# When the second layer's weight sums are made, and where its first outputs are copied, in an attention and two-MLP kernel

## The chip, the cores and the metric

The kernel runs on 1 core of one Trainium2 chip. The metric is the device time of one execution in microseconds (us). Engines are named as in the profile: PE (TensorE), DVE (VectorE), ACT (ScalarE), POOL (GpSimd) and SP (SyncE, which here only issues DMAs). Every engine and every DMA queue takes its instructions in the order in which they were laid down.

## The reference

Attention with a forget gate gives 2304 tokens of 512 values. Two MLPs follow, each with a hidden width of 2048:

```
x = attention(q, k, v, s)                          # 4 x 576 tokens, 8 heads of 64
h = x @ w_in1;  g = s1 * relu(h)**2 + b1;  x2 = g @ w_out1
h = x2 @ w_in2; g = relu(h) + alpha * min(h, 0);   out = g @ w_out2
```

## The kernel before

**Numbers.** All matrices are float32 in value. Each operand is split into a high and a low part (`split`: ACT copies the value into a rounded type, the high part; another engine, mostly DVE, subtracts to get the low part), and a product is three matmuls: high by high, high by low, low by high.

**Blocks.** Tokens go through a layer in blocks of 256. `SIZES` joins some: layer 0 (the first MLP) has seven single blocks and a wide one of 512 tokens (its matmuls write `hp` at L771 and `acc` at L882); layer 1 (the second MLP) has one single block, t=0, and then four wide ones, t=1 to 4. Every block has 16 steps f, one for each 128 hidden units: `up(f)` multiplies into PSUM, ACT and DVE apply the non-linear function and split the result into `gh` and `gl` (tiles `ring`), and `down(f)`, which is laid down two steps later in layer 0 and three in layer 1 (`LAG`), accumulates into the banks `acc`. `finish` copies the banks out.

**Packets.** The weights of layer 1 are loaded, converted (L140 on ACT, L141 and L142 on DVE) and split (L130 on ACT, L131 on DVE) in 16 packets while the wide block of layer 0 runs.

**Strassen.** The wide blocks of layer 1 save one product of eight: for two neighbouring steps, f and f+1 (one **pair**; there are 8), `up_first` makes three products in the PSUM banks a, b, c and `up_second` four more. Four of the seven left operands are sums of quarters of the weights. These sums don't depend on the tokens. `make_sums(pair)` makes them once: POOL adds ten times (L727; tiles `sum0` to `sum3`), then each of the four sums is split (ACT copy L130, DVE subtraction L131) into one of two halves of a small room, `rests` (in the rows the tiles `w1_0_0` with `w1_0_1`, and `w1_0_2` with `w1_0_3`), and written to DRAM (`sums_d`, two DMAs of 128 KB for each sum). Sums 0 and 2 share the first half and sums 1 and 3 the second, so each waits for the DMAs of the one ahead of it. `load_sums` brings a pair back into the tiles `sums` (L745, 256 KB for each sum) in every wide block, when `up_first` and `up_second` of the pair ahead have read the old ones.

**The order of the work.** The code is written in a program order, and a scheduler that works with modelled times lays the instructions down on each engine: an instruction may move ahead of others where the model has its operands ready and its engine free. `tc.issue_after(ins)` pins what is made inside it behind `ins` on that instruction's own engine. In program order, before, `make_sums` is called in block t=0 of layer 1 at f = 0, 3, 6, 9, 12, 15 and in block t=1 at f = 0 and 2; no pin holds its splits.

**The non-linear function of layer 1.** ACT makes the positive part `r` and the negative part `u` (tiles with the tags `ph` and `pl`, two buffers each), DVE merges them (`scalar_tensor_tensor`, L795 in block t=0 and L820 in the wide blocks), and `split` follows.

Of the kernel before, what the change touches and what calls it, by code (L numbers as in the profile page):

```python
# [12 lines left out]
AF = mybir.ActivationFunctionType  # L13
ALU = mybir.AluOpType
# [5 lines left out]
def tile_forget_attention__then__two_mlps(  # L20
# [20 lines left out]
    nc = tc.nc  # L41
# [6 lines left out]
    NF = DFF // P  # L48
# [13 lines left out]
    REBASE, W_SCALE = 2.0**-111, 2.0**8  # L62
# [22 lines left out]
    gate_s, gate_b, bsum, nalpha = misc[:, 0:1], misc[:, 1:2], misc[:, 4 : 4 + NCC], misc[:, 8 : 8 + NF]  # L85
# [43 lines left out]
    def split(hi, lo, src, lo_eng=nc.vector):  # L129
        nc.scalar.copy(hi, src)  # L130
        lo_eng.tensor_tensor(out=lo, in0=src, in1=hi.bitcast(F32), op=ALU.subtract)  # L131
# [14 lines left out]
    def slot(n, dtype, name):  # L146
        return wp.tile([P, 512], dtype, tag=f"w{n}", name=name)
# [560 lines left out]
        return {n: [x.rearrange("p (c n) -> p c n", c=2) for x in pair] for n, pair in parts.items()}, None  # L708

    ring, relus = [], []  # L710
    wide_ring, sums, sums_at = [], [], list(range(NF // 2))

    def halves(f):
        return [x.rearrange("p (k n) -> p k n", k=2) for x in (y.rearrange("p c n -> p (c n)") for y in packet(1, f)[:2])]
# [3 lines left out]
    def make_sums(pair):  # L718

        (h1, l1), (h2, l2) = halves(2 * pair), halves(2 * pair + 1)  # L720
        f32 = lambda x: x.bitcast(F32)
        add, sub = ALU.add, ALU.subtract

        def chain(n, first, *rest):
            out = one.tile([P, 2 * P], F32, tag=("ql00", "ql10", "ql11", "ql11")[n], name=f"sum{n}_{pair}")
            for m, (op, x) in enumerate(rest):
                nc.gpsimd.tensor_tensor(out=out, in0=out if m else f32(first), in1=f32(x), op=op)  # L727
            return out

        s1 = chain(0, h2[:, 0], (add, h2[:, 1]), (add, l2[:, 0]), (add, l2[:, 1]))  # L730
        s2 = chain(1, s1, (sub, h1[:, 0]), (sub, l1[:, 0]))
        s3 = chain(2, h1[:, 0], (sub, h2[:, 0]), (add, l1[:, 0]), (sub, l2[:, 0]))
        for n in range(4):
            s = chain(3, h1[:, 1], (sub, s2), (add, l1[:, 1])) if n == 3 else (s1, s2, s3)[n]
            hi, lo = rests[2 * (n % 2) : 2 * (n % 2) + 2]
            split(hi, lo, s)
            for z, part in enumerate((hi, lo)):
                nc.sync.dma_start(out=sums_d[pair, n, :, z * 2 * P : (z + 1) * 2 * P], in_=part.bitcast(F32))

# [8 lines left out]
    def mlp_block(layer, t, x):  # L748
# [5 lines left out]
        first, count = SIZES[layer][t]  # L754
# [5 lines left out]
        def up(f):  # L760
            w = packet(layer, f)
            if layer == 0 and count == 1:
                hp = ps_h.tile([P, 512], F32, tag="hp", name=f"hp{layer}_{t}_{f}")
            else:
                hp = ps.tile([P, 512], F32, tag="b", name=f"hp{layer}_{t}_{f}", bufs=4)
            hs = hp[:, :TB]
            terms = ((w[0], xh), (w[0], xl), (w[1], xh))
            n = 0
            for c in range(NCC):
                for a, b in terms:  # L770
                    nc.tensor.matmul(hs, a[:, c], b[c], start=(n == 0), stop=(n == len(terms) * NCC - 1))  # L771
                    n += 1
            if layer == 0 and count == 2:
                if not wide_ring:
                    tiles = [xfp.tile([P, 4, T], F32R, tag="xf", name=f"ring{n}") for n in range(3)]
                    for z in range(2):
                        wide_ring.append([x[:, 2 * z : 2 * z + 2].rearrange("p z n -> p (z n)") for x in tiles])
                gh, gl = (x[f % 3] for x in wide_ring)
                r = two.tile([P, TB], F32, tag="ph", name=f"r{t}_{f}")
            elif layer == 0:  # L780
                gh = two.tile([P, T], F32R, tag="gh", name=f"gh{layer}_{t}_{f}", bufs=3)
                gl = two.tile([P, T], F32R, tag="gl", name=f"gl{layer}_{t}_{f}", bufs=3)
                r = two.tile([P, T], F32, tag="r", name=f"r{t}_{f}")
            else:
                if not ring:
                    ring.extend([slot(n, F32R, f"ring{n}") for n in SPLIT[m]] for m in free[:2])
                gh, gl = (x[f % 4][:, :TB] for x in ring)
                r = two.tile([P, 512], F32, tag="ph", name=f"r1_{t}_{f}")[:, :TB]
                u = two.tile([P, 512], F32, tag="pl", name=f"u1_{t}_{f}")[:, :TB]
            relus.append(nc.scalar.activation(r, hs, AF.Relu, scale=1.0 / W_SCALE).ins)  # L790
            if layer == 0:
                nc.scalar.square(r, r)
            else:
                nc.scalar.activation(u, hs, AF.Relu, scale=-1.0 / W_SCALE)
                nc.vector.scalar_tensor_tensor(  # L795
                    out=r, in0=u, scalar=nalpha[:, f : f + 1], in1=r, op0=ALU.mult, op1=ALU.add
                )
            split(gh, gl, r, nc.gpsimd if layer == 0 and count == 1 else nc.vector)
            return gh, gl

# [11 lines left out]
        def next_sums(f, which):  # L812
            if f // 2 + 1 < NF // 2 or t + 1 < len(SIZES[1]):
                load_sums((f // 2 + 1) % (NF // 2), which)

        def temp(tag, name, bufs):
            return two.tile([P, T], F32, tag=tag, name=name, bufs=bufs)

        def prelu(r, u, f):
            nc.vector.scalar_tensor_tensor(  # L820
                out=r, in0=u, scalar=nalpha[:, f : f + 1], in1=r, op0=ALU.mult, op1=ALU.add
            )
            gh, gl = (y[f % 4][:, :TB] for y in ring)
            split(gh, gl, r)
            return gh, gl

        def relu_pair(r, u, src):
            nc.scalar.activation(r, src, AF.Relu, scale=1.0 / W_SCALE)
            nc.scalar.activation(u, src, AF.Relu, scale=-1.0 / W_SCALE)  # L829

        def up_first(f):
# [64 lines left out]

        def finish():
            for m, bank in enumerate(banks):
                if layer == 1 and count == 2:
                    res = two.tile([P, 512], F32, tag=("ph", "pl")[m % 2], name=f"res1_{t}_{m}")  # L900
                else:
                    if m % 2 == 0:
                        pool = xfp if m else one
                        both = pool.tile([P, 1024], F32, tag="xf" if m else "res", name=f"res{layer}_{t}_{m}")
                    res = both[:, m % 2 * 512 : (m % 2 + 1) * 512]
                if layer == 0:
                    for z in range(1 if count == 2 else 2):
                        d = m if count == 2 else 2 * m + z
                        dst, src = (res, bank) if count == 2 else (x[:, z * T : (z + 1) * T] for x in (res, bank))
# [4 lines left out]
                        else:  # L914
                            nc.vector.tensor_scalar(
                                out=dst, in0=src, scalar1=gate_s[:, 0:1], scalar2=bsum[:, d : d + 1],
                                op0=ALU.mult, op1=ALU.add,
# [5 lines left out]
                if layer == 0 and count == 2:  # L923
                    nc.sync.dma_start(
                        out=x2_d[first : first + 2, :, m * T : (m + 1) * T].rearrange("z p n -> p z n"),
# [46 lines left out]
    for n in range(len(BLOCKS) * NF):  # L972
# [18 lines left out]
            if n - NF * (len(SIZES[0]) - 1) == at:  # L991
                packet(1, j)
        if layer == 1:
            if sums_at and f % (2 if t else 3) == 0:
                make_sums(sums_at.pop(0))
        while done < len(units) and done < pace((n + 1) / NF):
            next(side, None)
# [39 lines left out]
```

## Time and profile before

| what | value |
|---|---|
| median of 3 runs | 1058.45 us (1057.36 to 1058.65) |
| the profiled execution | 1059.27 us, span 1057.5 us, mean granted clock 0.991 |
| PE busy | 1025.1 us, 97% of the span |
| DVE, ACT, POOL busy | 694.2, 673.9, 480.6 us |

The span runs from the first to the last instruction. Block t=0 of layer 1 begins on PE at 655.4 us of the span, block t=1 at 712.5 us, and its other three wide blocks follow. "idle" is the time for which an engine had nothing running ahead of an instruction, and "<-" names what ended it.

### The profile page before, as it was taken

How to read it: one execution, taken by the hardware profiler on the slowest of the kernel's cores; microseconds unless marked ns; L12 is line 12 of the kernel's file. 1: busy time of each engine (PE TensorE's matmuls, PEld its weight loads, DVE VectorE, ACT ScalarE, POOL GpSimd, SP SyncE). 2: the span in 40 equal slices, each digit the busy share in tenths (PEclk: the TensorE clock that was granted, in tenths of full speed). 3: DMA queues.
4: the chain of work that ended last, by engine and by line, in shares of the span. 5: the costliest groups of instructions: out<-in, count | busy, mean ns of one | idle time of the engine just before them, and what ended most of it. 6: DMA issues, size and time to landing. Idle time of an engine off the chain costs nothing.

```text
span 1057.5 us, 20662 instructions
## 1 busy us (share of the span) xinstructions
PE 1025.1 (97%) x6952; PEld 927.7 (88%) x6952; DVE 694.2 (66%) x1605; ACT 673.9 (64%) x1669; POOL 480.6 (45%) x892
## 2 busy tenths in 40 slices
PE   9899999999999999999999889799999999999997
PEld 4578899999999999999998667699999999999996
DVE  6888864786677766777557997945455446446443
ACT  5877866777778877877766665744454455445443
POOL 6556775666677666776644676512011002000000
PEclk9899999999999999999999999899999999999999
DMA  7998432342234332343126776514334335334331
GB/s 156 246 250 223 118 72 60 82 95 65 50 79 86 92 67 46 78 91 83 46 80 213 234 204 204 169 34 158 101 123 156 101 100 179 101 100 130 110 103 56
DMA packets 197930, 125.45 MB, mean 119 GB/s; under 512 B 138496, under 2 KB 167936, under 8 KB 197824
## 3 DMA queue, kind: packets, MB, share of 16 engines
q1 hardware_dynamic: 193744, 123.56, 42.5%
q8 instruction: 55, 0.90, 0.4%
q10 hardware_dynamic: 4080, 0.57, 0.3%
q14 instruction: 51, 0.42, 0.1%
HBM read 106.19 MB, written 17.90 MB: 117 GB/s over the span
## 4 chain that ended last, share of the span: by engine, by line
PE 76%; DVE 7%; DMA 7%; ACT 4%; issue 3%; POOL 2%; SPq 1%; ACTq 0%; DVEq 0%; POOLq 0%
PE acc L892 19%; PE p L807 15%; PE hp L771 15%; PE acc L882 13%; PE av L531 4%; PE pt L515 4%; PE sc L460 2%; DMA sums_d<-w 1%; DVE w L131 1%; PE sc L459 1%; DVE wt L142 1%; DMA wi<-in_moe_w_in_dram 1%; PE sc L457 1%; DMA wo<-in_moe_w_out_dram 1%; DVE wt L141 1%
## 5 line engine op out<-in xcount | busy, mean ns | idle before, releaser
L771 PE MATMUL hp<-xh,w 128*128 128x256 f32 (+1 forms) x1024 | 229.2, 301 | 0.6 <-ACT r L790 0.6
L892 PE MATMUL acc<-w,ring 128*128 128x512 f32 x864 | 215.6, 394 | 5.8 <-ACT res L911 5.8
L892 PEld LDWEIGHTS acc<-w,ring 128*128 128x128 f32 x864 | 157.6, 190 | 34.8 <-ACT res L911 6.0
L771 PEld LDWEIGHTS hp<-xh,w 128*128 128x128 f32 x1024 | 171.6, 190 | 6.6 <-ACT r L790 1.0
L882 PE MATMUL acc<-gh,w 128*128 128x256 f32 x896 | 172.3, 286 | 0.6 <-ACT res L911 0.5
L771 PE MATMUL hp<-xl,w 128*128 128x256 f32 (+1 forms) x512 | 152.6, 298 | 0.0
L868 POOL TENSOR_TENSOR cc<-u,t 128x256 f32<-128x256 f32 x32 | 25.7, 802 | 277.9 <-DVE u L859 241.6
L882 PEld LDWEIGHTS acc<-gh,w 128*128 128x128 f32 x896 | 136.0, 189 | 3.3 <-issue 1.3
L882 PE MATMUL acc<-gl,w 128*128 128x256 f32 x448 | 118.7, 288 | 1.4 <-POOL gl L131 1.4
L484 POOL TENSOR_SCALAR probs<-probs,sm 64x64 f32<-64x64 f32 (+4 forms) x160 | 91.3, 584 | 61.0 <-DVE sm L481 50.6
L473 ACT ACTIVATE probs<-probs,nm 64x64 f32<-64x64 f32 (+4 forms) x160 | 90.0, 563 | 37.8 <-DVE nm L461 26.1
L131 POOL TENSOR_TENSOR gl<-r,gh 128x256 fp32r<-128x256 f32 x112 | 89.5, 799 | 50.8 <-ACT gh L130 44.0
L807 PE MATMUL p<-xs,sums 128*128 128x256 f32 x768 | 103.9, 282 | 0.0
L771 PEld LDWEIGHTS hp<-xl,w 128*128 128x128 f32 x512 | 97.3, 190 | 3.4 <-issue 0.4
L807 PEld LDWEIGHTS p<-xs,sums 128*128 128x128 f32 x768 | 97.6, 189 | 1.0
L461 DVE CUSTOM_DVE_ANT_0 probs<-sc,probs 128x320 f32<-128x320 f32 (+3 forms) x160 | 68.2, 427 | 42.3 <-PE sc L460 27.7
L790 ACT ACTIVATE r<-hp 128x256 f32<-128x256 f32 (+1 forms) x144 | 58.0, 403 | 41.9 <-PE hp L771 31.3
L882 PEld LDWEIGHTS acc<-gl,w 128*128 128x128 f32 x448 | 80.1, 188 | 4.1 <-issue 2.0
L807 PEld LDWEIGHTS p<-xs,w 128*128 128x128 f32 x576 | 78.7, 189 | 5.4
L807 PE MATMUL p<-xs,w 128*128 128x256 f32 x576 | 81.3, 282 | 0.0
L515 PE MATMUL pt<-ident,probs 128*128 128x128 f32 x480 | 75.1, 277 | 4.2 <-POOL probs L484 2.4
L820 DVE SCALAR_TENSOR_TENSOR ph<-pl,misc,ph 128x512 f32<-128x512 f32 x64 | 48.6, 759 | 38.3 <-ACT pl L829 38.3
(149 smaller groups left out, 2160.7 us busy)
## 6 DMA issues: line engine op xcount, KB each, us to landing
sums<-sums_d SPq DMA_DIRECT2D x128, 256.0 KB, 2.7
wi<-in_moe_w_in_dram SPq DMA_DIRECT2D x32, 512.0 KB, 5.2
wo<-in_moe_w_out_dram SPq DMA_DIRECT2D x32, 512.0 KB, 5.3
cum<-cum_d SPq DMA_DIRECT2D x32, 288.0 KB, 3.7
sums_d<-w SPq DMA_DIRECT2D x64, 128.0 KB, 3.2
cum<-cum_d SPq DMA_DIRECT2D x30, 160.0 KB, 3.1
nat<-in_k_dram SPq DMA_DIRECT2D x64, 72.0 KB, 2.5
x_d<-res SPq DMA_DIRECT2D x18, 256.0 KB, 2.2
```

What stands on the lines that cost most here:

```text
L131: lo_eng.tensor_tensor(out=lo, in0=src, in1=hi.bitcast(F32), op=ALU.subtract)
L461: nc.vector.tensor_tensor_reduce(out=pt[:rows, j0:j1], in0=scr, in1=pt[:rows, j0:j1], scale=SCALE if flip else -SCALE, scalar=init, op0=AL ...
L473: nc.scalar.activation(pt[:rows, :n], pt[:rows, :n], AF.Exp, bias=nm[:rows, m : m + 1], scale=1.0 if flip else -1.0, accum_out=sm[:rows, m ...
L484: nc.gpsimd.tensor_scalar(out=probs[r][:rows, :n], in0=probs[r][:rows, :n], scalar1=sm[:rows, m : m + 1], scalar2=1.0, op0=ALU.mult, op1=A ...
L515: nc.tensor.transpose(tp[:, o : o + P], u.probs[h][r][:, k0 : k0 + P], ident)
L531: nc.tensor.matmul(av[:, nq - w : nq], lhs, part[:, o : o + w], start=(c == 0 and z == 0), stop=(c == last_c and z == len(parts) - 1), ski ...
L771: nc.tensor.matmul(hs, a[:, c], b[c], start=(n == 0), stop=(n == len(terms) * NCC - 1))
L790: relus.append(nc.scalar.activation(r, hs, AF.Relu, scale=1.0 / W_SCALE).ins)
L807: nc.tensor.matmul(bank, lhs[:, c * P : (c + 1) * P], rhs[:, c], start=(start and c == 0 and z == 0), stop=(c == 1 and z == 2), skip_group ...
L820: nc.vector.scalar_tensor_tensor(out=r, in0=u, scalar=nalpha[:, f : f + 1], in1=r, op0=ALU.mult, op1=ALU.add)
L882: nc.tensor.matmul(banks[d] if count == 2 else acc[d // 2][:, d % 2], a[:, d * P : (d + 1) * P], b, start=(f == 0 and (d % 2 == 0 or count ...
L892: nc.tensor.matmul(banks[m], a[:, m * P : (m + 1) * P], b, start=(f == 0 and b is woh and a is gh), stop=(f == NF - 1 and a is gl),)
```

## The change

`make_sums` is called at f = 8 and 12 of block t=0 and at f = 0, 2, 4, 6, 8 and 10 of block t=1. The splits of its sums are pinned behind the latest relu (on ACT) and the latest merge (on DVE) that program order has by then; for that the merges are collected in a list by a new function `merge`, and the relus of the wide blocks are added to theirs. The outputs of block t=0 of layer 1 are copied out through the tiles `ph` and `pl`, as those of the wide blocks were, and no longer through `res`.

```diff
-    wide_ring, sums, sums_at = [], [], list(range(NF // 2))
+    wide_ring, sums, sums_at, merges = [], [], list(range(NF // 2)), []
...
             hi, lo = rests[2 * (n % 2) : 2 * (n % 2) + 2]
-            split(hi, lo, s)
+            with tc.issue_after(relus[-1]), tc.issue_after(merges[-1]):
+                split(hi, lo, s)
...
                 nc.scalar.activation(u, hs, AF.Relu, scale=-1.0 / W_SCALE)
-                nc.vector.scalar_tensor_tensor(
-                    out=r, in0=u, scalar=nalpha[:, f : f + 1], in1=r, op0=ALU.mult, op1=ALU.add
-                )
+                merge(r, u, f)
...
+        def merge(r, u, f):
+            merges.append(
+                nc.vector.scalar_tensor_tensor(
+                    out=r, in0=u, scalar=nalpha[:, f : f + 1], in1=r, op0=ALU.mult, op1=ALU.add
+                ).ins
+            )
...
         def prelu(r, u, f):
-            nc.vector.scalar_tensor_tensor(
-                out=r, in0=u, scalar=nalpha[:, f : f + 1], in1=r, op0=ALU.mult, op1=ALU.add
-            )
+            merge(r, u, f)
...
         def relu_pair(r, u, src):
-            nc.scalar.activation(r, src, AF.Relu, scale=1.0 / W_SCALE)
+            relus.append(nc.scalar.activation(r, src, AF.Relu, scale=1.0 / W_SCALE).ins)
...
-                if layer == 1 and count == 2:
+                if layer == 1:
                     res = two.tile([P, 512], F32, tag=("ph", "pl")[m % 2], name=f"res1_{t}_{m}")
...
-            if sums_at and f % (2 if t else 3) == 0:
+            if sums_at and (f % 2 == 0 if t else f in (8, 12)):
                 make_sums(sums_at.pop(0))
```

What the scheduler makes of it: the instructions of every engine stand as before up to the middle of layer 0's wide block, and again from step 11 of block t=1 on. Between, PE's order is the same but for the interleaving of some products in block t=1. In the names below, `sum1_3` is sum 1 of pair 3, `ring` the tiles of gh and gl, `r7_5` the relu of step 5 of layer 0's wide block, and `wt6_0` the first half of packet 6.

**Place 1, DVE in the wide block of layer 0.** These rows lead up to the subtraction that ends step 5. Before:

```order
L131 TENSOR_TENSOR w1_4_9_9426<-wt4_1_9431,w1_4_10_9425 128x512
L131 TENSOR_TENSOR w1_0_1_9218<-sum0_1_10167,w1_0_0_9217 128x256
L131 TENSOR_TENSOR w1_5_11_9474<-wt5_0_9477,w1_5_12_9473 128x512
L131 TENSOR_TENSOR w1_0_3_9220<-sum3_0_10020,w1_0_2_9219 128x256
L141 TENSOR_SCALAR wt5_1_9481<-wt5_1_9481 128x512
L141 TENSOR_SCALAR wt6_0_9557<-wt6_0_9557 128x512
L142 SCALAR_TENSOR_TENSOR wt5_1_9481<-wo1_5_9470,wt5_1_9481 128x512
L141 TENSOR_SCALAR wt6_1_9561<-wt6_1_9561 128x512
L142 SCALAR_TENSOR_TENSOR wt6_0_9557<-wi1_6_9549,wt6_0_9557 128x512
L142 SCALAR_TENSOR_TENSOR wt6_1_9561<-wo1_6_9550,wt6_1_9561 128x512
L131 TENSOR_TENSOR ring2_9195<-r7_5_9452,ring2_9195 128x512
```

The same stretch of the changed kernel:

```order
L131 TENSOR_TENSOR w1_4_9_9426<-wt4_1_9431,w1_4_10_9425 128x512
L131 TENSOR_TENSOR w1_5_11_9474<-wt5_0_9477,w1_5_12_9473 128x512
L141 TENSOR_SCALAR wt6_0_9557<-wt6_0_9557 128x512
L142 SCALAR_TENSOR_TENSOR wt6_0_9557<-wi1_6_9549,wt6_0_9557 128x512
L141 TENSOR_SCALAR wt6_1_9561<-wt6_1_9561 128x512
L142 SCALAR_TENSOR_TENSOR wt6_1_9561<-wo1_6_9550,wt6_1_9561 128x512
L131 TENSOR_TENSOR w1_6_19_9554<-wt6_0_9557,w1_6_20_9553 128x512
L131 TENSOR_TENSOR ring2_9195<-r7_5_9452,ring2_9195 128x512
```

The subtractions of the sums are gone; the packets' work stays.

**Place 2, ACT at the seam of the layers.** `res0_7` are the copies of layer 0's last banks, `r1_0_2` and `u1_0_2` the relus of step 2 of block t=0. Before:

```order
L130 CAST w1_14_60_10063<-wt14_0_10067 128x512
L790 ACTIVATE r1_0_2_10092<-hp1_0_2_10079 128x256
L794 ACTIVATE u1_0_2_10093<-hp1_0_2_10079 128x256
L911 ACTIVATE res0_7_0_10111<-acc0_7_1_9177,misc_90 128x512
L130 CAST w1_0_0_9217<-sum0_7_10833 128x256
```

The same place of the changed kernel:

```order
L130 CAST w1_14_60_10033<-wt14_0_10037 128x512
L791 ACTIVATE r1_0_2_10062<-hp1_0_2_10049 128x256
L915 ACTIVATE res0_7_0_10081<-acc0_7_1_9177,misc_90 128x512
L795 ACTIVATE u1_0_2_10063<-hp1_0_2_10049 128x256
L130 CAST w1_14_62_10035<-wt14_1_10041 128x512
```

The copy of the bank now stands ahead of `u1_0_2`, and the sum's copy behind it is gone.

**Place 3, DVE in block t=1 of layer 1.** `u3` and `u2` read PSUM bank b and bank c of a pair. Before, no sum is left here:

```order
L820 SCALAR_TENSOR_TENSOR ph2_1_3_10902<-pl2_1_3_10903,misc_90,ph2_1_3_10902 128x512
L131 TENSOR_TENSOR ring58_9988<-ph1_1_3_10863,ring38_9984 128x512
L131 TENSOR_TENSOR ring57_9989<-ph2_1_3_10902,ring37_9985 128x512
L859 TENSOR_TENSOR u3_1_5_10966<-p1_1_4_10924,t1_1_4_10926 128x256
L863 TENSOR_TENSOR u2_1_4_10928<-p2_1_4_10925,u2_1_4_10928 128x256
```

The changed kernel, from the same merge to the same reads:

```order
L817 SCALAR_TENSOR_TENSOR ph2_1_3_10783<-pl2_1_3_10784,misc_90,ph2_1_3_10783 128x512
L131 TENSOR_TENSOR w1_0_1_9218<-sum0_4_10845,w1_0_0_9217 128x256
L848 TENSOR_TENSOR u2_1_4_10809<-p1_1_4_10805,t1_1_4_10807 128x256
L131 TENSOR_TENSOR w1_0_3_9220<-sum3_3_10737,w1_0_2_9219 128x256
L131 TENSOR_TENSOR ring57_9989<-ph2_1_3_10783,ring37_9985 128x512
L131 TENSOR_TENSOR w1_0_3_9220<-sum1_4_10849,w1_0_2_9219 128x256
L863 TENSOR_TENSOR u3_1_5_10877<-p1_1_4_10805,t1_1_4_10807 128x256
L867 TENSOR_TENSOR u2_1_4_10809<-p2_1_4_10806,u2_1_4_10809 128x256
```

Three subtractions of sums of two pairs now stand ahead of `u3_1_5`, two of them one behind the other in the same half of `rests`.

## Rows read from the trace of the kernel before

**Rows 1.** By stage: us, busy PE, PEld, DVE, ACT, POOL, clock, DMA share, GB/s.

```profile
565.00:593.00 28.00, 28.00 (x123) 22.81 (x123) 26.60 (x40) 20.93 (x43) 19.80 (x19) 1.00 0.76 246
593.00:682.00 89.00, 72.35 (x312) 55.94 (x311) 78.02 (x106) 55.50 (x112) 58.15 (x61) 0.94 0.67 203
682.00:712.00 30.00, 30.00 (x192) 27.11 (x191) 16.68 (x34) 13.58 (x40) 4.57 (x5) 1.00 0.18 58
712.00:784.00 72.00, 72.00 (x466) 65.74 (x465) 36.00 (x63) 31.98 (x76) 9.34 (x11) 1.00 0.37 117
```

**Rows 2.** What PE waited for from 560 us on: total, times, longest.

```profile
PE acc L882 <- DVE ring L131: 7.9, 6, 2.7
PE acc L892 <- ACT res L911: 5.8, 1, 5.8
```

**Rows 3.** Timeline of PE: start, us, instructions, idle before them.

```profile
582.77 2.95 PE L882 MATMUL acc<-ring,w 128*128 128x512 f32 x12
585.56 0.39 PE L771 MATMUL hp<-xh,w 128*128 128x512 f32 x1
...
591.08 0.39 PE L771 MATMUL hp<-xh,w 128*128 128x512 f32 x1
...
597.15 2.59 PE L882 MATMUL acc<-ring,w 128*128 128x512 f32 x10 [2.71 <-DVE ring L131]
...
655.38 0.28 PE L771 MATMUL hp<-xgh,w 128*128 128x256 f32 x1
...
674.77 3.27 PE L892 MATMUL acc<-w,ring 128*128 128x512 f32 x6 [5.77 <-ACT res L911]
...
681.25 0.28 PE L771 MATMUL hp<-xgh,w 128*128 128x256 f32 x1
...
682.69 1.56 PE L892 MATMUL acc<-w,ring 128*128 128x512 f32 x6
```

**Rows 4.** The same columns right behind the longest wait.

```profile
675.00:678.00 3.00, 3.00 (x7) 2.04 (x8) 3.00 (x5) 2.47 (x6) 2.61 (x4) 0.50 0.83 228
```

**Rows 5.** Timeline of DVE: Place 1's first row, the one behind it, two without POOL.

```profile
586.83 1.23 DVE L131 TENSOR_TENSOR w<-wt,w 128x512 fp32r<-128x512 f32 x1
...
597.02 0.41 DVE L131 TENSOR_TENSOR w<-sum,w 128x256 fp32r<-128x256 f32 x1
...
653.41 0.42 DVE L141 TENSOR_SCALAR wt<-wt 128x512 uint32<-128x512 uint32 x1
653.87 0.69 DVE L142 SCALAR_TENSOR_TENSOR wt<-wo,wt 128x512 uint32<-128x512 uint32 x1
```

**Rows 6.** DVE by form, 586 to 680 us: count, busy us, mean ns.

```profile
L131 DVE TENSOR_TENSOR w<-sum,w 128x256 fp32r<-128x256 f32 x26 | 16.6, 646 | 5.1 <-ACT w L130 5.0
L131 DVE TENSOR_TENSOR ring<-r,ring 128x512 fp32r<-128x512 f32 x12 | 11.3, 944 | 2.4 <-ACT ring L130 2.4
```

**Rows 7.** DVE by form, 740 to 784 us, with hardly any POOL work.

```profile
L131 DVE TENSOR_TENSOR ring<-ph,ring 128x512 fp32r<-128x512 f32 x9 | 6.2, 692 | 5.5 <-ACT ring L130 5.5
```

**Rows 8.** POOL by form, 565 to 691 us: the commonest of the sums' ten additions.

```profile
L727 POOL TENSOR_TENSOR sum<-sum,w 128x256 f32<-128x256 f32 x56 | 52.2, 949 | 4.7 <-DVE w L131 2.9
```

**Rows 9.** Timeline of ACT: the copies of sum1_1 and sum1_4, then the seam.

```profile
592.45 0.41 ACT L130 CAST w<-sum 128x256 fp32r<-128x256 f32 x1 [0.33 <-POOL sum L727]
...
631.62 0.40 ACT L130 CAST w<-sum 128x256 fp32r<-128x256 f32 x1
...
673.67 0.38 ACT L794 ACTIVATE u<-hp 128x256 f32<-128x256 f32 x1 [2.03 <-DVE w L131]
673.95 0.77 ACT L911 ACTIVATE res<-acc,misc 128x512 f32<-128x512 f32 x1
```

**Rows 10.** The sums' ten writes and loads issued from 676 to 700 us.

```profile
DMA to landing us min/median/max: 1.7/2.4/3.8
```

**Rows 11.** The chain that ended last, block t=1: start, us, work.

```profile
744.91 2.15 PE p L807 x18
...
755.39 2.15 PE p L807 x18
```

## The prediction

> **Bound.** I read four views, in this order. The busy time by stage [rows 1] says where PE loses time: in layer 1's blocks PE is busy for all of 30.00 and 72.00 us, and from 565 to 593 us for all of 28.00. Only between 593 and 682 us, the second half of layer 0's wide block and the seam of the layers, is it idle, for 89.00 - 72.35 = 16.65 us. The change moves instructions in this stage and behind it, up to about 770 us, and nothing elsewhere.
>
> The waits of PE [rows 2] name VectorE's `ring` subtractions (7.9 us in six waits) and one copy of the banks (5.8 us). In the timeline of PE [rows 3] the reader is to see what they cost in steps. An undisturbed step of the wide block takes 591.08 - 585.56 = 5.52 us. From 591.08 to 655.38 there are nine steps: 64.30 us where 9 x 5.52 = 49.7 would do, 14.6 lost. From 655.38 to 681.25 PE does five `up` of 12 matmuls with 256 columns (1.44 each, 681.25 to 682.69) and 36 matmuls with 512 columns (2.79 for 12, 582.77 to 585.56): 15.6 us of work in 25.87, 10.3 lost. Together **24.9 us**. It is more than the idle time, because behind the wait of 5.77 us the granted clock is 0.50 [rows 4], the lower of the two levels, and matmuls take twice as long.
>
> The timeline of DVE says why. The rows of Place 1 run without a gap from 586.83 to 597.02, where the row behind them starts [rows 5]: 10.2 us for work that has to fit into little more than one step of 5.52. PE starts again at 597.15, right behind the `ring` row that ends them [rows 3]. Two things fill DVE: the sums' own subtractions (26 of them, 16.6 us, [rows 6]), and rows that take longer beside POOL's additions. The same subtraction of 128x512 has a mean of 944 ns here [rows 6] and 692 where POOL hardly works [rows 7]; the first row of Place 1, the same operation, takes 1.23 [rows 5].
>
> **Removed.** All 32 splits of sums leave this stage, and POOL's chains go with them, since their tiles are free only after the splits: eight of its 80 additions stay, those that stand before the first split. What is left to DVE in one step is 0.69 for `ring` [rows 7] and, as packets come every 1.25 steps, 2 x (0.42 + 0.69 + 0.69) / 1.25 = 2.9 us [rows 5], so 3.6 of 5.52. Place 1 of the changed kernel is eight rows that take some 5.0 us by those prices instead of 10.2. At the seam, `u1_0_2` waited 2.03 us for its buffer, and the copy of the bank was queued behind it [rows 9]; now the copy is ahead (Place 2). Behind its last `down`, PE still has 17 matmuls to do before it needs the bank, about 2.0 us, and an undelayed copy takes 0.77 [rows 9]. I take **-24.9 us** for the stage, and keep **+1** (0 to 3) for what can still be late at the seam: the last two packets' conversions stand ahead of the copy on DVE, and PE will now come there sooner. The weights' loads lose the sums' writes ahead of them in SP's queue.
>
> **Added.** The same 32 splits, 80 additions and 64 writes now lie beside blocks that have had no idle time.
>
> Block t=0, pairs 0 and 1: 8 copies and 8 subtractions of 0.41 [rows 5, 9] in 30 us in which ACT is busy 13.58 and DVE 16.68 [rows 1]. The copy of sum 2 waits for sum 0's DMA, and a relu queued behind it comes some 3 us late. The `down` that needs it stands three steps behind its `up`, 3 x (1.44 + 1.40) = 8.5 us, and the five short instructions between take 2.5. Cost 0; with that cover gone it would be those 3 us for each pair.
>
> Block t=1, pairs 2 to 7, one for each 10.48 us (744.91 to 755.39, [rows 11]). Load: DVE works 36.00 / 72 x 10.48 = 5.2 us for a pair [rows 1] and gets 4 x 0.41 more. That fits. Order: each half of `rests` is used twice for a pair, and one use is a copy 0.41, a subtraction 0.41 to 0.65 [rows 5, 6], SP's issue 0.3 and a landing of 2.4 to 3.8 us [rows 10], so 3.5 to 5.2; two make 7.1 to 10.3, just inside 10.48. But they hold others up. ACT waits with a copy until the half is free, and relus stand behind it; in Place 3 `u3_1_5` is behind the subtraction of sum1_4, which needs the DMA of sum3_3 of the same half. Following one pair through with 4.1 us for each use, `u3` and the relus come 2 to 4.5 us late, while PE has other matmuls for 3.5 to 4.8 us before it needs the bank back (for `u3_1_5`, 18 of 256 columns and 6 of 512: 18 x 0.12 + 6 x 0.23 = 3.5). So some pairs cost nothing and some up to 1.5 us. The loads of `sums` stand behind writes of the next pair in SP's queue, and are 1 to 2 us ahead of their use. I take half a microsecond for each of six pairs, **+3**; the bounds are 0 (every use 3.5 us) and 7.8 (first rival).
>
> Outputs through `ph` and `pl`: no instruction more. Two later tiles of step 3 now wait for two writes of 256 KB. These stand in SP's queue behind loads that are due some 5 us before those tiles, more than the longest landing of 3.8 [rows 10], so 0; late, they would cost such a landing once. `res` is free for the next block's operands.
>
> **Sum.** 1059.27 of the profiled execution - 24.9 + 1 + 3 = 1038.4. The median of the runs is 0.8 lower than that execution, so **1037.6 us**, 2.0% faster. Alone, this case spans 1033.0 (nothing added) to 1041.
>
> **A rule.** The same rows of 944 and 692 ns [rows 6, 7] say that VectorE loses 0.25 us for a row beside POOL. In block t=1 two merges, two `ring` rows and four sums' subtractions of each pair would lie beside ten additions: 8 x 0.25 = 2.0 us, and DVE has 5.2 + 1.6 + 2.0 = 8.8 of 10.48. The Trainium skill, "SBUF — State Buffer", section "Who interferes with whom", says that VectorE and GpSimd hold their shared ports under an exclusive lock for a whole instruction, and the other blocks. Taken at its word, each of the eight would wait a whole addition; that is the third rival. The trace shows a mean of a quarter of that.
>
> **Rivals.** The first: the chain through `rests` sets the pace of block t=1. Before, from sum1_1 to sum1_4, three pairs took 39.17 us [rows 9], 13.1 each. At that pace six pairs take 15.7 us more than PE's 62.9; a pair is asked for two pairs ahead of its use, 21 us, of which its own 13.1 leave 7.9. So PE waits 7.8 us and the time is about 1042.5. For it: the chain is the same. Against: there the conversions shared ACT and DVE.
>
> The second: the wide block stays short of DVE or of weights. If half of the 24.9 us comes from the packets themselves, the time is 1050. Against: from 565 to 593 us PE had no idle time with packets and sums together [rows 1].
>
> The third, slower: POOL locks DVE out in block t=1. Each of the eight rows waits 0.949 us [rows 8]: 5.2 + 1.6 + 7.6 = 14.4 us for a pair, 3.9 over PE's 10.48, 24 us over six pairs; with the clock at its lower level after the waits (some 3 us, as behind the one wait of [rows 4]), nothing is won: about 1060. It decides from 0.9 us for each row on. Against: the 0.25 measured.
>
> That the pins do nothing is excluded by the orders shown.
>
> **Chances.** My forecast 0.69, the first rival 0.17, the second 0.08, the third 0.06 (slower 0.04, same 0.02). Faster than before by over 0.2% (2.1 us, about what a measurement of this kernel can tell) is 0.69 + 0.17 + 0.08 = 0.94; same 0.02; slower 0.04. The range that leaves out no more than 2 in 10 goes from 1033.0 into the first rival's case, with 3 us at the seam on top: 1045.5.
>
> **Signs.** In the profile after: no idle PE from 593 us to the seam, step after step at 5.52; `ring` rows at 0.69; a clock of 1.00 at the seam, and a wait there of under 2 us; no copy of a sum before step 8 of block t=0, which begins some 24 us earlier. In block t=1 waits of PE of under 1.5 us on `u3`, on `p` or on `sums`, 3 us in all, and DVE rows lengthened beside POOL. It is wrong if the steps of the wide block stay over 6 us, or if block t=1 takes more than 92 us instead of 84.

## The result and the profile after

The changed kernel takes a median of **1042.15 us** in four runs (1039.45 to 1047.4), beside 1058.17 for the kernel before: a ratio of 0.9855, 95% interval [0.9815, 0.9896]. Run again on another occasion it took 1039.65 us (experiment 1), a ratio of 0.981 [0.9784, 0.9836]. The prediction was 1037.6, with a range of 1033.0 to 1045.5.

The windows of the profile after, by stage, answer to [rows 1] (us, then busy us and count of PE, PEld, DVE, ACT and POOL, granted clock, DMA share, GB/s):

```profile
593.00:657.00 64.00, 64.00 (x304) 53.28 (x304) 42.86 (x76) 44.94 (x82) 0.00 (x0) 1.00 0.49 156
644.67:691.39 46.72, 46.72 (x296) 42.14 (x294) 34.42 (x63) 28.48 (x74) 16.58 (x20) 1.00 0.40 125
691.39:733.39 42.00, 40.71 (x263) 36.48 (x262) 31.72 (x49) 20.51 (x54) 37.28 (x43) 1.00 0.67 202
733.39:754.39 21.00, 19.10 (x112) 16.29 (x110) 14.93 (x22) 10.47 (x26) 16.33 (x19) 1.00 0.64 199
754.39:775.39 21.00, 21.00 (x134) 19.01 (x133) 14.56 (x27) 12.96 (x29) 4.16 (x5) 1.00 0.47 147
```

From 593 us to the seam and over it PE has no idle time, the clock is 1.00, and POOL does nothing: the loss of [rows 1] is gone. Block t=0 (644.67 to 691.39) is full as well. The idle time that PE still has between 593 us and its last matmul is all in block t=1, 3.2 us of its first 63, and in those 63 us POOL is busy for 53.6.

The timeline of PE after, at one step of the wide block and at the seam (start, us, instructions):

```profile
583.88 0.39 PE L772 MATMUL hp<-xh,w 128*128 128x512 f32 x1
...
589.40 0.39 PE L772 MATMUL hp<-xh,w 128*128 128x512 f32 x1
...
641.88 2.96 PE L886 MATMUL acc<-ring,w 128*128 128x512 f32 x12
644.67 0.28 PE L772 MATMUL hp<-xgh,w 128*128 128x256 f32 x1
```

A step takes 589.40 - 583.88 = 5.52 us, as the undisturbed one of [rows 3]. The timeline of DVE after has the eight rows of Place 1 of the changed kernel (two of them joined):

```profile
589.59 1.29 DVE L131 TENSOR_TENSOR w<-wt,w 128x512 fp32r<-128x512 f32 x2
591.02 0.43 DVE L141 TENSOR_SCALAR wt<-wt 128x512 uint32<-128x512 uint32 x1
591.48 0.69 DVE L142 SCALAR_TENSOR_TENSOR wt<-wi,wt 128x512 uint32<-128x512 uint32 x1
592.61 0.43 DVE L141 TENSOR_SCALAR wt<-wt 128x512 uint32<-128x512 uint32 x1 [0.43 <-ACT wt L140]
593.07 0.69 DVE L142 SCALAR_TENSOR_TENSOR wt<-wo,wt 128x512 uint32<-128x512 uint32 x1
593.68 0.68 DVE L131 TENSOR_TENSOR w<-wt,w 128x512 fp32r<-128x512 f32 x1
594.28 0.68 DVE L131 TENSOR_TENSOR ring<-r,ring 128x512 fp32r<-128x512 f32 x1
```

They take 5.4 us, a wait of 0.43 for ACT among them, where the eleven rows of before took 10.2 [rows 5]. What PE waits for in block t=1 (total, times, longest), and the timeline of PE at two of these waits:

```profile
PE p L806 <- DVE u L863: 1.5, 3, 1.0
PE p L806 <- ACT t L846: 0.9, 1, 0.9
PE p L806 <- DVE u L848: 0.7, 1, 0.7
```

```profile
733.66 2.89 PE L896 MATMUL acc<-w,ring 128*128 128x512 f32 x12
737.47 0.98 PE L806 MATMUL p<-xs,w 128*128 128x256 f32 x6 [0.92 <-ACT t L846]
738.29 1.78 PE L806 MATMUL p<-xs,sums 128*128 128x256 f32 x12
...
742.63 0.87 PE L806 MATMUL p<-xs,w 128*128 128x256 f32 x6
744.47 0.98 PE L806 MATMUL p<-xs,w 128*128 128x256 f32 x6 [0.97 <-DVE u L863]
745.29 1.59 PE L806 MATMUL p<-xs,sums 128*128 128x256 f32 x12
```

L863 is `u3`. Where PE doesn't wait, six matmuls of 256 columns take 0.71 us from start to start (1022.26 to 1022.97 in the same profile), so the product of 744.47 was due at 742.63 + 0.71 = 743.34. It came 1.13 us late, and the group behind it, at 745.29, another 0.11, for a wait listed as 0.97. Loss is therefore read from starts below, not from the sum of waits.

The same four marks, read from the timeline of PE, stand for every kernel: its first `hp` product, the first one with 512 columns (the wide block), the first of block t=0 and of block t=1, and the start of the last group of `p` products. Times in us:

| kernel | first hp | wide to t=0 | t=0 to t=1 | t=1 to last p | median of runs |
|---|---|---|---|---|---|
| before | 60.41 | 101.72 | 57.11 | 331.98 | 1058.17 |
| changed | 64.13 | 87.16 | 46.72 | 337.11 | 1042.15 |

From the wide block to block t=1 the change wins 24.95 us. The last stretch, t=1 to t=4, gives back 5.13; since PE has no idle time behind the first 63 us of it, this is called the loss of block t=1.

### The profile page after: what moved, and what is told of

It is laid out like the page before. It is cut to its first block, busy times and chain, and to the rows that moved or that the text cites. A ratio compares the mean times of both kernels' runs of the same rounds, so it can differ in the third digit from the quotient of the medians.

```text
span 1041.2 us, 20629 instructions
## 1 busy us (share of the span) xinstructions
PE 1021.4 (98%) x6952; PEld 927.0 (89%) x6952; DVE 686.3 (66%) x1605; ACT 672.7 (65%) x1669; POOL 468.1 (45%) x892
## 4 chain that ended last, share of the span: by engine, by line
PE 77%; DMA 5%; POOL 5%; ACT 4%; DVE 4%; issue 3%; SPq 1%; ACTq 0%; DVEq 0%; POOLq 0%
PE hp L772 18%; PE acc L896 16%; PE acc L886 16%; PE p L806 13%; PE pt L515 4%; PE av L531 4%; POOL sum L727 2%; PE sc L460 2%; DMA vn<-in_v_dram 1%; PE sc L459 1%; DMA sums_d<-w 1%; DMA wo<-in_moe_w_out_dram 1%; PE acc_first L97 1%; PE sc L457 1%; POOL probs L484 1%
## 5 line engine op out<-in xcount | busy, mean ns | idle before, releaser
L473 ACT ACTIVATE probs<-probs,nm 64x64 f32<-64x64 f32 (+4 forms) x160 | 90.0, 563 | 37.8 <-DVE nm L461 25.7
L817 DVE SCALAR_TENSOR_TENSOR ph<-pl,misc,ph 128x512 f32<-128x512 f32 x64 | 52.7, 823 | 38.2 <-ACT pl L833 38.0
```

Source lines behind the costliest of these rows:

```text
L473: nc.scalar.activation(pt[:rows, :n], pt[:rows, :n], AF.Exp, bias=nm[:rows, m : m + 1], scale=1.0 if flip else -1.0, accum_out=sm[:rows, m ...
L817: nc.vector.scalar_tensor_tensor(out=r, in0=u, scalar=nalpha[:, f : f + 1], in1=r, op0=ALU.mult, op1=ALU.add).ins
```

## The experiments

Eleven kernels ran, each timed beside the kernel before on the same chip: experiments 1 to 4 on one chip, 5 to 8 on a second, 9 to 11 on a third. "Loss" is the excess over 87.16, 46.71 and 331.98 us, the shortest of each stretch. The edits are given against the changed kernel, unless said otherwise.

| kernel | first hp | wide to t=0 | t=0 to t=1 | t=1 to last p | median us | ratio to before |
|---|---|---|---|---|---|---|
| again | 60.52 | 87.17 | 46.71 | 337.38 | 1039.65 | 0.981 [0.9784, 0.9836] |
| no_pins | 59.51 | 101.93 | 56.29 | 332.00 | 1061.1 | 1.0021 [0.9996, 1.0046] |
| old_outputs | 59.94 | 87.16 | 46.72 | 337.62 | 1040.95 | 0.982 [0.9794, 0.9845] |
| pins_old_times | 62.91 | 87.16 | 52.68 | 339.36 | 1050.55 | 0.9914 [0.9883, 0.9946] |
| before_no_adds | 61.34 | 89.61 | 53.71 | 331.98 | 1043.89 | 0.986 [0.9836, 0.9884] |
| after_no_adds | 59.40 | 87.17 | 46.71 | 332.15 | 1035.73 | 0.9784 [0.9758, 0.981] |
| four_halves | 60.84 | 87.17 | 46.71 | 335.74 | 1038.99 | 0.9804 [0.978, 0.9829] |
| three_early | 61.30 | 87.16 | 46.93 | 339.80 | 1042.95 | 0.9847 [0.9826, 0.9869] |
| idle_adds | 61.30 | 87.16 | 46.72 | 336.49 | 1038.89 | 0.9811 [0.9777, 0.9845] |
| eight_adds | 60.24 | 87.16 | 46.72 | 334.09 | 1036.38 | 0.9775 [0.9749, 0.9801] |
| eight_halves | 60.34 | 87.16 | 46.72 | 332.07 | 1035.26 | 0.9766 [0.974, 0.9792] |

**1. The changed kernel again** (no edit).

> The changed kernel unchanged, to see where its spread of 8 us (1039.5 to 1047.4) lies. Theory: ahead of the change. The first profile had column sums at 155.0 us where before had 158.8, so the start differs from execution to execution, and from the first product of block t=0 to the end the program takes the same time. Then the median is 1042 (1038 to 1047), the stretch from the first product of t=0 (644.67 in the first profile) to the last is 396.5 within 1 us, and the wide block's steps are 5.52. Rival: the spread lies in block t=1, where waits of half a microsecond to 1.5 us start the clock's lower level in some executions; then the stretch from 644.67 on differs by several us and the start does not.

From the first product of block t=0 to the end of the span it is 396.5 us in the first profile and 1037.7 - 640.92 = 396.8 in this one. The first `hp` product came at 64.13 there and at 60.52 here, 3.6 us earlier, and the two spans differ by 3.5 (1041.2 and 1037.7). So the difference arose ahead of this mark, in the attention's start, where the engines' orders are those of before. The thirteen profiles have the mark between 59.4 and 64.1 us. The theory holds for these two profiles. Where the slowest run, 1047.4, lost its time no profile shows.

**2. Without the pins.**

```diff
-            with tc.issue_after(relus[-1]), tc.issue_after(merges[-1]):
-                split(hi, lo, s)
+            split(hi, lo, s)
```

> Sums asked for at the new steps, but their splits not pinned; outputs through ph and pl. The scheduler then puts all 27 splits back into the wide block, in the order of before, and every engine's instructions are as before but for the outputs of block t=0. Theory (the pins carry the change): 1058.2 within 2 us, the steps of the wide block lose 14 us and the seam 10, as in rows 3. Rival (the outputs' room carries part of it): at least 4 us faster than before, 1054 or less.

All of the gain is gone: 101.93 us to block t=0 and 56.29 to block t=1, within 0.8 us of before. The median, 1061.1, is above the 1058.2 within 2 that was expected, but the kernel before had 1060.15 beside it. What PE waits for between 552 and 712 us in this kernel answers to [rows 2]:

```profile
PE acc L885 <- DVE ring L131: 8.3, 7, 2.4
PE acc L895 <- ACT res L914: 5.7, 1, 5.7
```

Asking later does nothing by itself, since the scheduler puts the splits back into the wide block. The outputs through `ph` and `pl`, which this kernel has, bring nothing either.

**3. Outputs through `res`.**

```diff
-                if layer == 1:
+                if layer == 1 and count == 2:
                     res = two.tile([P, 512], F32, tag=("ph", "pl")[m % 2], name=f"res1_{t}_{m}")
```

> The changed kernel with the outputs of block t=0 copied through res as before; the scheduler shifts some splits of pairs 3 to 6 by a merge or two. Theory (the outputs' path costs and brings nothing): within 2 us of the changed kernel, 1040 to 1044. Rival (res holds up the next block's operands): 3 to 8 us slower, 1045 to 1050, with a wait of POOL or DVE for res in block t=1.

The stretches agree with experiment 1 within 0.24 us. The outputs' path neither costs nor brings anything; its one use is that `res` is free, which experiments 7, 10 and 11 need.

**4. Pins, but asked for at the old steps.**

```diff
-            if sums_at and (f % 2 == 0 if t else f in (8, 12)):
+            if sums_at and f % (2 if t else 3) == 0:
```

> Pins, but the sums asked for at the old steps: 20 splits (five pairs) now stand in block t=0, none in the wide block. Theory (the wide block needs DVE free, and the chain through rests needs 7 to 10 us for a pair): the wide block's steps are 5.52 and its gain of 14 us stays, but five pairs take 35 to 50 us where block t=0 has 28, and relus stand behind the copies, so 7 to 20 us are lost there: 1049 to 1062. Rival (the pins alone do it, the steps at which the sums are asked for don't matter): 1042 within 3 us.

The wide block keeps its gain (87.16). Block t=0, which now has five pairs, gets 6.0 us longer, and block t=1 2.0 longer than in experiment 1. So the pins make the gain and the later steps keep 8 us of it. The loss in t=0 is below the 7 to 20 that were expected of it; with that in t=1, 7.4, the median comes out in the range all the same.

**5. The kernel before, without POOL's additions** (against the kernel before).

```diff
-            out = one.tile([P, 2 * P], F32, tag=("ql00", "ql10", "ql11", "ql11")[n], name=f"sum{n}_{pair}")
-            for m, (op, x) in enumerate(rest):
-                nc.gpsimd.tensor_tensor(out=out, in0=out if m else f32(first), in1=f32(x), op=op)
-            return out
+            return f32(first)
```

> The kernel before without POOL's ten additions for each pair: plain quarters of the weights are split and written in the sums' place, so the second layer's outputs are not the reference's. 28 splits stay in the wide block. Theory (DVE overflows there because rows take longer beside POOL: 0.944 instead of 0.692 us, 0.646 instead of 0.41): Place 1's eleven rows take 6.2 us instead of 10.2, the wide block loses under 4 us instead of 14.6, its ring rows are at 0.69, and the time is 1038 to 1048. Rival (the number of DVE's rows, or the sums' DMAs ahead of the packets' loads, are enough): the wide block still loses 8 us or more, 1050 or more.

DVE by form in the wide block, with all the splits but no POOL (count, busy us, mean ns):

```profile
L131 DVE TENSOR_TENSOR w<-w,w 128x256 fp32r<-128x256 f32 x25 | 10.1, 423 | 14.0 <-DMA sums_d<-w 13.9
L141 DVE TENSOR_SCALAR wt<-wt 128x512 uint32<-128x512 uint32 x21 | 8.9, 424 | 3.2 <-ACT wt L140 3.0
L131 DVE TENSOR_TENSOR ring<-r,ring 128x512 fp32r<-128x512 f32 x12 | 8.3, 689 | 2.5 <-ACT ring L130 2.4
```

The same rows had means of 646 (sums) and 944 ns (`ring`) in [rows 6]. With as many rows on DVE, the wide block loses 2.45 us instead of 14.56. So 12 of the 14.6 are POOL's doing. That it does this by making DVE's rows long is read from DVE's load: from the wide block to block t=0 it is busy 85.5 us with 119 rows before, and 61.6 us with 120 rows here. The edit also takes away ACT's waits for the sums, 8.2 us before; the two are not tested apart. The splits with their DMAs account for the other 2.5, and for 7.0 of the 10.4 us at the seam, where PE again waits 3.2 us for the copy into `res`.

**6. The changed kernel without the additions** (the same edit).

> The changed kernel with the same cut: no additions, plain quarters split in the sums' place, outputs not the reference's. In the two profiles of the changed kernel block t=1 loses 5.3 us (first product of t=1 to the last product: 337.1 and 337.4 us, 332.0 before). Theory (the chain through rests, with its DMAs, makes u3 and the copies late): at least 3.5 us of the 5.3 stay. Rival (POOL makes the sums late and DVE's rows long): under 1.5 us stay, 1034 to 1036 if the changed kernel has 1039.7.

Block t=1 loses 0.17 us instead of 5.13 to 5.40. ACT and DVE do wait for the sums' writes there, 9.6 and 7.7 us in all, but PE waits for nothing. So without the additions the 32 splits, the 64 writes and the chain through `rests` cost next to nothing; **the theory fell**. What block t=1 pays it pays only with POOL's additions beside it.

**7. A second room for the sums.**

```diff
+        rooms = rests + rests
+        if pair > 1:
+            more = one.tile([P, 1024], F32R, tag="res", name=f"more_{pair}")
+            rooms = rests + [more[:, i * 2 * P : (i + 1) * 2 * P] for i in range(4)]
...
-            hi, lo = rests[2 * (n % 2) : 2 * (n % 2) + 2]
+            hi, lo = rooms[2 * n : 2 * n + 2]
```

> The changed kernel with a second room for the sums of pairs 2 to 7: sums 0 and 1 go through the two halves of rests as before, sums 2 and 3 through the tile res, which the changed kernel no longer needs for outputs, so each half is used once for a pair instead of twice. Theory (chain through rests): no wait for a write of the same pair is left, block t=1 loses under 2 us instead of 5.3, and the time is 3 to 5 us below the changed kernel, 1034 to 1037. Rival (DVE's load beside POOL, or POOL's additions themselves, make u3 late): it still loses 4 us or more, 1038.5 to 1041.

The loss in t=1 is 3.76 us: neither under 2 nor over 4, with a median in the rival's range. The second use of each half costs 1.4 to 1.6 of the 5.1 to 5.4. ACT still waits for POOL's sums, 17.8 us in nine waits, and what PE waits for is now mostly ACT's copy `t` of a product (1.0 of 1.3 us) instead of `u3`.

**8. Three pairs asked for in block t=0.**

```diff
-            if sums_at and (f % 2 == 0 if t else f in (8, 12)):
+            if sums_at and (f % 2 == 0 if t else f in (4, 8, 12)):
```

> The changed kernel with sums asked for at f = 4, 8 and 12 of block t=0 and five times in t=1: four pairs' splits stand in block t=0 instead of three, and four in t=1 instead of five. Theory (loss goes by pairs beside t=1, and block t=0 from step 4 on has room for pairs of 8 us): block t=0 keeps its 46.7 us from its first product to that of t=1, t=1 loses 3.5 to 4.5 us instead of 5.3, 1038 to 1040. Rival (the last packets' conversions leave no room at step 4): t=0 gets 2 to 5 us longer, 1041 to 1045.

Neither: block t=0 is as short as ever (46.93), and t=1 loses 7.8 us although fewer additions lie beside it (47 instead of 53). So the number alone doesn't set the loss. The timeline of ACT shows one of PE's six waits:

```profile
698.27 0.40 ACT L130 CAST w<-sum 128x256 fp32r<-128x256 f32 x1 [3.57 <-POOL sum L727]
698.58 0.38 ACT L832 ACTIVATE ph<-p 128x256 f32<-128x256 f32 x1
698.86 0.38 ACT L833 ACTIVATE pl<-p 128x256 f32<-128x256 f32 x1
```

The copy waits 3.57 us for POOL's sum, and the relus of the block's first pair stand behind it; PE then waits 0.83 us for the second of them. The changed kernel has such a wait too, of 3.91 us, but it ends 7.5 us behind the start of block t=1 and not 10.4, and PE doesn't wait. Why the sums come later here stays open, and so does how the other five waits arise.

**9. Additions that nobody reads.** The ten additions of pairs 3 to 7 stay on POOL, pinned behind its latest `cc`; plain quarters are split.

```diff
+                with tc.issue_after(ccs[-1]):
                     nc.gpsimd.tensor_tensor(out=out, in0=out if m else f32(first), in1=f32(x), op=op)
...
+            s = f32((h2[:, 0], h2[:, 1], h1[:, 0], h1[:, 1])[n])
```

> The changed kernel in which POOL still makes the ten additions of pairs 3 to 7 beside block t=1 (each pinned behind POOL's own latest cc), but nobody reads them: the splits take plain quarters of the weights, as in after_no_adds, and the outputs are not the reference's; pairs 0 to 2 have no additions. It keeps POOL busy and the rows beside it long, and takes away every wait for a sum. Theory (the sums come late, because ten additions of 0.88 us and one cc fill POOL's 10.48 us for a pair): block t=1 loses under 1.5 us (first product of t=1 to the last under 333.5 us), though DVE's ring rows keep a mean of 0.85 us or more there. Rival (the long rows themselves make u3 late): 3 us or more, 335 or more.

Block t=1 loses 4.5 us although no split waits for a sum: the rival. The splits' waits for writes are short as well (1.9 us on ACT, 1.4 on DVE). The timeline of DVE ahead of the longest wait of PE (1.06 us) shows the cause:

```profile
733.80 0.93 DVE L819 SCALAR_TENSOR_TENSOR ph<-pl,misc,ph 128x512 f32<-128x512 f32 x1 [0.95 <-ACT pl L835]
734.66 1.84 DVE L131 TENSOR_TENSOR w<-w,w 128x256 fp32r<-128x256 f32 x2
736.42 1.22 DVE L131 TENSOR_TENSOR ring<-ph,ring 128x512 fp32r<-128x512 f32 x1
737.56 1.82 DVE L131 TENSOR_TENSOR w<-w,w 128x256 fp32r<-128x256 f32 x2
739.30 0.41 DVE L865 TENSOR_TENSOR u<-p,t 128x256 f32<-128x256 f32 x1
```

Without a gap, six rows take 5.5 us until `u3` (L865) starts. Their mean prices without POOL's additions are 0.79 (the merge, in after_no_adds), 4 x 0.42 and 0.69, 3.2 us. POOL is denser here than in the changed kernel (10.3 to 10.5 busy of 10.5 us in four windows), so 4.5 us may be more than the long rows cost there.

**10. Eight additions instead of ten** (pairs 2 to 7).

```diff
+            put(a, h2[:, 0], l2[:, 0], add)
+            put(b, h2[:, 1], l2[:, 1], add)
+            put(b, b, a, add)
+            put(d, h1[:, 0], l1[:, 0], add)
+            put(c, b, d, sub)
+            put(a, d, a, sub)
+            put(d, h1[:, 1], l1[:, 1], add)
+            put(d, d, c, sub)
+            four = b, c, a, d
```

> The changed kernel with eight additions instead of ten for pairs 2 to 7, the same sums: h2+l2 and h1+l1 of a quarter are made once and used twice (the fourth sum then needs a tile of its own, for which res is free). Theory (POOL's 10 x 0.88 + 0.85 = 9.65 of 10.48 us for a pair is what makes the sums late): POOL needs 7.9, t=1 loses 1 to 3 us instead of 5.3, the time is 2 to 4 us below the changed kernel, 1035.5 to 1037.5. Rival (the chain through rests, or the number of rows that meet an addition): it loses 4.5 us or more, 1039 to 1041.

Block t=1 loses 2.1 us, as the theory had it, and one wait of PE of 1.1 us is left.

**11. Eight additions and the second room.** Both edits; `d` is a tile with the tag `r`.

> Both edits: eight additions for pairs 2 to 7 and the second room of four_halves in res (the fourth sum's tile is one of the 128x256 tiles r). If the two causes add up, four_halves' 1.6 us and eight_adds' 1 to 4 us leave 0 to 2 us of loss in t=1: 332.0 to 334.0 us from its first product to the last, 1034 to 1036. If one of them is the only limit, it equals the better of the two others within 0.5 us.

The causes add up: block t=1 takes 332.07 us, 0.09 over the kernel before. From the first `hp` product to the last `p` product it is 959.89 us, 4.6 under experiment 1's 964.49. With a ratio of 0.9766 it is faster than the kernel before. Against the changed kernel, timed on another chip (0.981), the intervals of the ratios overlap slightly, so that it is faster than this one rests on the 4.6 us of the profiles. Three of its windows in block t=1:

```profile
698.66:709.16 10.50, 10.50 (x71) 9.63 (x70) 8.66 (x15) 6.24 (x16) 8.96 (x11) 1.00 0.73 228
709.16:719.66 10.50, 10.50 (x68) 9.46 (x67) 9.35 (x14) 5.09 (x14) 9.54 (x11) 1.00 0.82 253
719.66:730.16 10.50, 10.50 (x68) 9.52 (x67) 8.08 (x15) 7.39 (x19) 8.54 (x10) 1.00 0.63 209
```

PE is full, though DVE's `ring` rows still have a mean of 0.973 us there. Long rows alone, with POOL a little short of full and no wait for a write, are not enough to make `u3` late.

## Why the prediction was right, and which term was off

**The stage, -24.9 + 1.** Measured -24.95 in both profiles of the changed kernel, with nothing left at the seam: steps of 5.52, `ring` rows with a mean of 0.688, Place 1 in 5.4 us for a predicted 5.0. The reason stood too. Experiment 2 shows that the place of the splits is all of it, and experiment 5 divides it: most of what the wide block lost came of POOL's additions, which lengthen DVE's rows; the prediction named this as the second of "two things" that fill DVE. It is the larger one by far in the block, and the splits and their DMAs matter mainly at the seam. The kept +1 was not needed.

**Block t=1, +3.** Measured +5.1 and +5.4, within the bounds of 0 and 7.8, but 1.7 to 1.8 times the term. Two steps were wrong in it. The idle time was foreseen well, 3.1 us for 3, but a wait costs PE more than its idle record: the 3.1 us moved the products by 5.1. And the path was incomplete: the prediction timed each use of `rests` and let DVE's rows lengthen, but it never added up POOL's own load. At the prices before, ten additions of 0.949 [rows 8] and a `cc` of about the same price are 10.4 us for PE's 10.48. After, at the prices below, they are 9.6, and POOL also makes operands of the blocks: it is busy 37.28 of the first 42 us. Against that, DVE's load came out as worked out (7.4 to 9.0 us of 10.5 in five windows of a pair each, from 701.89 to 754.39 us, for a predicted 8.8 of 10.48), and a write of a sum landed in 1.9 us in the median, less than the 2.4 to 3.8 that were priced. POOL by form in block t=1 after:

```profile
L727 POOL TENSOR_TENSOR sum<-sum,w 128x256 f32<-128x256 f32 x38 | 32.8, 874 | 1.6
L872 POOL TENSOR_TENSOR cc<-u,t 128x256 f32<-128x256 f32 x8 | 7.1, 887 | 15.6 <-ACT xs L130 9.5 <-DVE u L863 6.1
```

What Place 3 showed is there. In the timeline of DVE after, 2.22 us of idle time ahead of the last split of Place 3 end with the write of `sum3_3`, as the prediction had it, and PE then loses 0.45 us to `u3_1_5`; the dearer wait comes two pairs later, where `u3` again has three splits ahead of it:

```profile
720.99 0.73 DVE L131 TENSOR_TENSOR w<-sum,w 128x256 fp32r<-128x256 f32 x1 [2.22 <-DMA sums_d<-w]
721.64 0.41 DVE L863 TENSOR_TENSOR u<-p,t 128x256 f32<-128x256 f32 x1
...
738.51 1.02 DVE L817 SCALAR_TENSOR_TENSOR ph<-pl,misc,ph 128x512 f32<-128x512 f32 x1 [0.49 <-ACT pl L833]
739.45 0.96 DVE L131 TENSOR_TENSOR w<-sum,w 128x256 fp32r<-128x256 f32 x1
740.97 1.01 DVE L131 TENSOR_TENSOR w<-sum,w 128x256 fp32r<-128x256 f32 x1 [0.56 <-DMA sums_d<-w]
741.91 1.22 DVE L131 TENSOR_TENSOR ring<-ph,ring 128x512 fp32r<-128x512 f32 x1
743.66 0.43 DVE L131 TENSOR_TENSOR w<-sum,w 128x256 fp32r<-128x256 f32 x1 [0.53 <-DMA sums_d<-w]
744.00 0.42 DVE L863 TENSOR_TENSOR u<-p,t 128x256 f32<-128x256 f32 x1
```

There `u3` starts 5.5 us behind the merge (738.51); 1.1 us of this are waits for the sums' writes, the rest is rows, most of them long. A third part lies on ACT, for PE's wait of 0.92 us at 737.47: the copy `t` that PE needs is queued behind a sum's copy that waits for POOL.

```profile
736.74 0.41 ACT L130 CAST w<-sum 128x256 fp32r<-128x256 f32 x1 [1.81 <-POOL sum L727]
737.05 0.37 ACT L846 COPY t<-p 128x256 f32<-128x256 f32 x1
```

In all, ACT waits 12.4 us for POOL's sums beside block t=1, in seven waits. All three parts need POOL's additions: without additions the same splits and writes cost 0.17 us (experiment 6), with eight additions 2.1, with a second room 3.8, with both 0.09. How much of the changed kernel's own 5.1 to 5.4 us each part costs by itself stays open, since each edit also shifts when the other falls due.

**The rivals.** The first, that `rests` sets the pace, would have cost 7.8 us, and the changed kernel loses 5.1 to 5.4. In experiment 6 the chain, whole but without POOL's sums in it, costs 0.17 us, and in experiment 7, where each half is used once for a pair, 1.4 to 1.6 us come back. So it is a part of the path and doesn't set the pace. The second, that half of the stage's loss stays, is excluded by the steps of 5.52. The third, that each row waits a whole addition, did not come: `ring` rows in t=1 have a mean of 0.956 us, an excess of 0.27, not 0.949. A whole addition for every row was the most that such a lock could cost, since under it a row that comes while an addition runs waits only for what is left of that addition. It was the right place, though: 2.2 of PE's 3.1 us of waits in block t=1 are for DVE.

**The sum.** From the first `hp` product to the last `p` product the prediction's terms give 984.06 - 20.9 = 963.2 us; the profiles have 964.37 and 964.49. For a profiled execution they gave 1038.4. The first one has 1043.1: 1.2 more in the terms, and 64.13 - 60.41 = 3.7 ahead of the first `hp` product, a part of the program that no term covers. That the terms agree so well is in part luck: the +1 that wasn't needed made up for nearly half of what the term of block t=1 lacked. The part ahead of the first `hp` product differs so between the two profiles of the same kernel, which may be why the medians of 1042.15 and 1039.65 differ. The lower end of the range is no exact sum: with nothing added it is 1059.27 - 24.9 - 0.8 = 1033.6, not 1033.0.

**The other signs** came. The relu of step 8 of block t=0 starts at 670.37 us and the first copy of a sum right behind it, at 670.96; before, that relu stood at 692.33, so it comes 22.0 us earlier, and 25.7 in the second profile (666.61). At the seam `res` waits for no buffer. Block t=1 takes 5.1 us more than 84, under the 92 that would have refuted the term.

## What to carry to other kernels

When work moves into a full stage, add up the load of every engine that it brings along, the one that only helps included: here DVE and the buffers were checked, and POOL, at 9.6 to 10.4 of 10.48 us, was not. A pin that keeps work out of a saturated stage can be worth more than the choice of step at which it is asked for, and a scheduler without the pin undoes that choice. Before an addition is moved, see whether it is needed: two of ten were not, and that with one freed tile won 4.6 us more.

## What the runs showed of the hardware

**Which DVE rows POOL lengthens.** DVE by form in block t=1 after, with POOL busy for most of it:

```profile
L131 DVE TENSOR_TENSOR w<-sum,w 128x256 fp32r<-128x256 f32 x24 | 15.8, 671 | 9.4 <-ACT w L130 4.0 <-DMA sums_d<-w 4.0 <-ACT pl L833 1.4
L131 DVE TENSOR_TENSOR ring<-ph,ring 128x512 fp32r<-128x512 f32 x14 | 13.4, 956 | 2.9 <-ACT ring L130 2.8
L863 DVE TENSOR_TENSOR u<-p,t 128x256 f32<-128x256 f32 x8 | 3.3, 416 | 0.0
```

Rows with both inputs in SBUF go from 423 to 671 and from 689 to 956 ns. The additions of `u3`, with one input in PSUM, stay at 416; in the quiet blocks of the kernel before they took 424. The Trainium skill, "SBUF — State Buffer", section "Who interferes with whom", says just this: a VectorE instruction with two SBUF inputs contends with a GpSimd instruction that reads SBUF, and one with at most one SBUF input, outside the faster two-port modes, does not. The trace agrees. L141 has one input too, and its mean in the wide block of the kernel before, 753 ns, is above the 424 of experiment 5, at which it is faster than a row of two inputs with as many columns (`ring`, 689). The same section of the Trainium skill names this operation, `tensor_scalar`, among those that can enter such a mode when their operands allow it; no row shows the mode itself. The two rows of the kernel before, 586 to 680 us and 745 to 1040 us:

```profile
L141 DVE TENSOR_SCALAR wt<-wt 128x512 uint32<-128x512 uint32 x21 | 15.7, 753 | 1.5 <-ACT wt L140 1.5
```

```profile
L859 DVE TENSOR_TENSOR u<-p,t 128x256 f32<-128x256 f32 x29 | 12.3, 424 | 39.3 <-PE p L807 39.3
```

**How much.** The excess is much the same for a row of 0.42 and of 0.69 us: about a quarter of a microsecond in the mean. In the second profile of the changed kernel the `ring` rows lie between 0.69 and 1.27, so none took more than 0.58 longer, less than the 0.73 of POOL's shortest additions. POOL pays as well: its additions there that stand alone in the timeline range from 0.73 to 1.19 us.
